# A's tile with its seven column groups side by side, late chunks' copies on ScalarE, and another written order, in a chunked RWKV-7 kernel with a SwiGLU feed-forward

## The chip, the core and the metric

The kernel runs on one core of one Trainium2 chip. The metric is the device time of one execution in microseconds, taken as the median of several runs. The core has five engines that run side by side, each through its own instruction list in order: TensorE (PE in the profile; its weight loads are PEld), VectorE (DVE), ScalarE (ACT), GpSimd (POOL) and SyncE (SP), of which SP only issues transfers. Transfers are also issued from POOL's queue.

## The reference

```python
# r, k, v, w, a, b: (B, H, S, D) = (4, 8, 768, 40), one state (D, D) per batch and head
for t in range(S):
    y[:, :, t] = einsum('bhd,bhde->bhe', r_t, state)
    Sa = einsum('bhde,bhe->bhd', state, a_t)
    state = state * w_t[:, :, None, :] - einsum('bhd,bhe->bhde', Sa, b_t) \
            + einsum('bhd,bhe->bhde', v_t, k_t)
x = y as (B*S, H*D) = (3072, 320)
xn = x / sqrt(mean(x*x) + 1e-6) * rms_g
out = (silu(xn @ w_gate) * (xn @ w_val)) @ w_out      # d_ff = 1536
```

All arithmetic is in 32-bit floats. The three weight matrices come in as 64-bit floats.

## The kernel before

The 768 steps are cut into 24 chunks of 32. The 32 pairs of batch and head lie side by side: `N = 8` slots times two halves, `NI = 16` on the free axis, the rest on the partitions.

`narrow` turns a weight slice's 64-bit words into 32-bit floats (three ACT passes and three DVE operations each for 24 half slices) and writes them to `sW` in memory, from which the feed-forward loads its tiles `wf`.

`front(c)` prepares chunk `c`: it loads and turns w, a, k and b. From them it builds products of decays `T`, the scaled keys `K` and the scaled `a` columns, and the matrix `LT` of what each step of the chunk does to later ones. `LT` is filled by distance. Columns up to three steps apart, within groups of four, come from one matmul group ("gramk") of `K` with the tile `A`; the levels 4, 8 and 16 come from three more with the tile `Ab`. For each of the 8 groups of four columns `A` has seven: the three a columns 1 to 3, two of them times a decay, and one of those times two; so its shape is [128, 16, 8, 7], the seven of a group next to each other. Line 742 (ACT) fills the first three, lines 751 and 752 (DVE) the others. Three masked copies (`where`, lines 757 to 760) take the product's columns for distance 1, 2 and 3 into `LT`, three, two and one column of each group. Line 770 (DVE) makes part of `Ab` from `A`.

`inverse(c)` inverts the chunk's triangular matrix: 31 steps of two small DVE operations each (`tmp`, `Yi`), with transfers before and after it. Chunks below `EARLY` use another form.

`main(c)` runs the chunk: "state" and "lower" matmuls, `Xs` (ACT), "lower" again into U, four copies of U into `VU` by half and slot group, "update" of the state, the turning of `VU`, "score", the masked scores `As` (one operation per level), "level" matmuls, sums into `y`, then the normalisation and the turn into `xg`. Some of these operations go to another engine from chunk `LATE` on.

`feed(g)` is the feed-forward for two chunks: six rounds of "h64", "h" (gate and value), Silu on ACT, a product on DVE (`hT`) and "out", summed in the PSUM tile `po`.

What comes when is written out by hand in ORDER. Every operation is a piece, numbered as the code makes it; a word of ORDER is a piece's number counted from the first piece not yet issued, so the words give each engine's order. A "-" issues a warm-up matmul (line 1079) on the identity into spare columns of `po`. PAIRS says for each PSUM room which of the three PSUM pairs it takes. Pieces wait for the pieces whose data they use, wherever these stand.

Of the kernel before, what the change touches and what calls it, by code (L numbers as in the profile page):

```python
# [17 lines left out]
P = 128  # L18
# [4 lines left out]
EARLY, LATE = 4, 6  # L23
# [10 lines left out]
4 5 6 7 8 9 10 11 - - 46 - - - - 43 53 18 - 316 323 58 - - 61 47 60 525 27 44 - - - - 12 13 14 15 16 17 19 317  # L34
- - 313 315 324 314 333 327 328 - 318 325 - 326 - - 73 339 - 74 85 93 84 - 94 82 83 334 337 - 336 335 338 -
340 349 20 21 22 350 355 23 342 343 24 25 26 - 367 - 354 348 - 352 - 344 345 363 346 365 347 - - 351 75 76 362
353 360 628 397 29 - 443 455 - 452 442 36 32 56 - 48 38 59 54 31 441 35 456 - 636 - 451 444 - 62 453 446 33 -
454 - 37 70 45 - 626 445 - 41 638 356 125 122 - 1 332 331 321 103 322 113 114 329 - 95 86 98 379 359 78 79 364
87 361 374 366 - 376 - 378 - - - - 373 77 357 368 371 377 375 387 372 89 88 358 - 461 - 386 369 383 90 80 -
380 381 465 370 466 384 - - 99 463 464 462 470 341 - 91 471 - - 478 - - 481 482 - 385 467 395 468 477 - - 476  # L40
- 483 493 480 - 389 391 390 - - 104 392 81 394 393 105 123 102 472 490 479 627 633 64 42 50 398 448 34 - 623 -
57 67 624 55 - 459 49 634 460 449 52 65 457 51 635 637 - - 473 - 474 491 - 475 450 - - 625 96 492 - 97 396 494
- - 489 - 504 382 100 487 488 - 484 506 - - 399 400 495 401 - 402 403 503 404 - - - 485 496 405 406 407 500
408 409 - 410 505 - 411 - 412 413 414 415 416 507 417 418 497 419 516 420 421 643 422 423 424 - 499 425 426
427 428 - 106 644 - - 502 501 498 107 108 429 124 320 0 317 90 576 - 132 577 - 328 99 643 645 511 510 - 484 -
113 646 644 509 107 - - - - 506 - 507 - 512 658 - 386 650 651 - 663 467 675 - - - 108 116 - 109 662 428 647
516 517 518 515 131 - 521 114 648 124 522 - 657 508 - - - 652 429 578 567 524 - - 61 870 456 861 860 - 640 66
445 430 69 - 598 871 26 - 28 64 639 630 67 629 110 519 520 434 656 - 653 - 654 661 - 117 660 659 127 128 - 655
580 - 115 - - 674 - - 579 513 664 - - - 432 143 431 433 118 525 526 670 568 125 126 669 133 581 666 134 135
435 436 437 438 569 141 142 140 119 687 129 - 668 673 667 161 152 151 163 - 665 144 527 528 529 136 137 138  # L50
679 530 531 532 533 671 534 535 536 537 147 676 160 130 573 571 572 570 672 682 145 146 684 148 538 680 539
540 541 542 543 544 545 546 547 548 149 549 550 685 551 552 553 - 554 582 583 686 - 574 153 555 575 681 156
677 162 139 801 164 678 586 688 167 157 689 - 589 595 590 - 604 693 154 165 155 690 587 588 596 1 0 962 135
145 144 113 146 134 663 519 661 662 560 136 137 143 612 121 122 660 556 557 555 646 554 712 520 664 665 562
129 138 655 147 148 149 563 131 564 568 565 132 569 - 713 566 832 668 33 - 827 841 826 825 - - 837 521 - 835
669 842 828 836 838 0 830 524 522 523 165 521 164 714 656 658 569 138 653 713 669 670 671 - 672 570 673 149
674 571 - 572 675 676 677 678 525 842 526 847 846 843 845 844 - 848 527 153 154 132 162 665 528 715 163 962
139 679 680 150 140 174 141 681 151 682 859 683 684 685 851 849 858 666 852 863 686 687 688 853 717 719 716
718 155 166 156 857 861 689 854 864 690 855 158 691 860 159 856 169 876 157 - 160 850 862 - 692 - 869 722 720
723 - - 546 764 182 - 152 183 185 173 167 547 726 573 168 875 574 - 721 - 575 729 731 865 1009 1008 - 600 -  # L60
1019 599 1018 1016 576 866 693 888 730 735 867 738 737 694 734 732 193 161 184 577 657 175 727 578 728 736 874
695 696 697 868 698 699 871 - 870 739 186 963 733 170 171 - 966 964 - 176 965 177 - 187 873 188 746 745 178
179 740 952 741 742 743 744 - 877 883 879 882 700 194 - - 579 881 880 747 180 872 887 886 172 195 885 580 748
582 - 878 889 891 581 884 749 750 751 752 753 829 590 589 1010 1020 896 754 892 - 890 1026 1013 1027 205 701
202 203 1021 1012 - 1022 - 1023 702 828 1028 705 703 950 951 755 - - 1011 894 893 838 756 1017 0 725 726 576
15 851 850 577 848 772 16 852 849 855 864 17 714 8 - 9 10 18 856 857 578 580 867 - 869 581 525 1093 579 19 23
33 719 720 32 853 723 854 868 862 863 877 866 879 523 717 0 573 515 575 516 713 869 517 847 707 710 711 574 42
0 509 5 839 840 845 841 707 861 567 753 850 14 754 855 856 755 893 568 708 709 569 570 757 853 710 - 711 8 17
851 712 713 714 715 716 717 718 854 719 871 523 21 23 22 867 852 858 756 - 872 - 766 868 524 - 866 869 873 720
# [4 lines left out]
776 876 877 878 18 879 880 881 882 883 884 885 748 - - 871 749 872 - - 1073 944 945 1078 1077 1075 1076 1074  # L74
23 560 719 561 1079 720 562 563 5 6 7 1082 1083 8 - 1090 886 887 1095 1093 1106 1080 947 564 0 12 715 24 - 712
556 13 16 1080 714 23 713 0 878 879 880 0 0 1072 875 1068 709 550 1069 1075 1070 876 1078 1087 877 710 10 1085
11 18 0 1073 1081 1080 9 875 1068 548 549 - - 708 - 1077 709 - 1085 1083 1079 - 929 758 759 876 1086 0 926
1077 17 1087 549 550 22 992 0 15 14 1193 12 542 543 544 765 1239 764 1250 1033 775 1043 867 868 869 1052 750
870 1090 871 872 1082 751 1240 920 1085 752 923 1089 1099 873 1083 874 875 876 1088 9 877 878 879 922 1084 921
545 1079 926 546 880 881 882 0 1085 1079 15 5 18 926 882 0 15 16 5 1079 545 546 1089 928 - 547 - - 548 - - -  # L80
939 1090 882 883 884 8 885 886 887 888 889 890 930 1093 1085 751 1091 929 1094 941 549 551 550 552 937 935 936
18 931 1092 19 891 932 553 938 940 892 893 894 895 896 897 933 898 899 900 942 554 555 1099 1098 1100 9 1101
972 - 0 1170 1083 1084 1085 0 196 546 - 0 0 385 343 344 551 - 386 - 345 552 376 346 - - 387 349 347 415 348
350 354 353 352 351 364 365 390 - 196 195 548 388 549 197 389 553 - 537 554 555 556 557 558 559 560 561 562
563 391 392 393 394 395 - 564 565 566 567 568 569 570 571 572 573 574 575 576 577 396 273 634 637 636 635 0 0
0 0 - 617 393 394 - 0 0 0 615 691 676 463 675 686 680 690 674 687 682 685 684 677 474 571 572 573 574 575 392
576 577 578 579 580 581 582 583 584 585 586 587 588 589 590 591 592 593 464 393 394 395 617 361 362 692 698
396 695 694 - 696 697 693 - - - 398 397 399 758 701 702 712 - 618 400 401 402 616 709 714 594 595 596 597 699
# [339 lines left out]
def kernel(  # L428
# [78 lines left out]
    def tt(o, a, b, op):  # L507
        dve("tt", nc.vector.tensor_tensor, o, a, b, op)
# [603 lines left out]
```

## Time and profile before

| | |
|---|---|
| runs, median of 3 | 1048.17 us (1045.47 to 1050.28) |
| profiled execution, span from first to last instruction | 1035.9 us |
| median of the runs less the span | 12.3 us |
| mean granted TensorE clock | 0.972 |
| instructions | 56007 |
| PE busy, matmuls | 989.6 us, 96% |
| DVE busy | 832.1 us, 80% |
| ACT busy | 450.8 us, 44% |
| POOL busy | 309.1 us, 30% |
| transfers from memory and back | 93.39 MB and 15.99 MB |
| copy of the first and the last group's `po` | at 232.3 and 1030.8 us |

The profiled execution's time is known only as its span; the 12.3 us are what lies around the span by the runs. Rows of instruction groups read: line, engine, operation, out<-in, shapes, count | busy us, mean ns of one | idle us just before them and what ended it. Rows of windows read: from:to, length, busy us of the engines (with counts), granted clock, share of the transfer engines, GB/s. Rows of the chain and of the timeline begin with the start and the length in us. All operations of one helper have its line: 505 is any DVE operation, 528 an ACT copy, 531 an ACT scaling, 547 a matmul, 550 a turn.

### The profile page before, as it was taken

Reading aid. Unit: us, or ns where it says so; the run is one execution under the profiler, and the core shown is the slowest. Engines: PE = TensorE matmul, PEld = TensorE weight load, DVE = VectorE, ACT = ScalarE, POOL = GpSimd, SP = SyncE. Lnnn points to the kernel's source line nnn. Section 1 sums busy time; section 2 is a strip of 40 time slices with the busy share of each in tenths; the row PEclk is TensorE's granted clock in tenths of the full one; section 3 lists DMA queues with packets and bytes.
Section 4 is the critical chain, followed back from the end, with each engine's and each line's share of the span. In section 5 each row is a group of like instructions: output and inputs, shape, how many; then the busy total and the mean of one; then the engine's idle time right before and its main releaser. Section 6 shows DMA issues by size and latency. Waiting matters only on the chain.

```text
span 1035.9 us, 56007 instructions
## 1 busy us (share of the span) xinstructions
PE 989.6 (96%) x24842; PEld 807.6 (78%) x24842; DVE 832.1 (80%) x2789; ACT 450.8 (44%) x1019; POOL 309.1 (30%) x554
## 2 busy tenths in 40 slices
PE   7987999999999999999999999999999999999998
PEld 7976877788887787787877787887787877778876
DVE  8987688686869899899989888888799898788410
ACT  5784775543553443443443433452434444341210
POOL 9633413041442233232244232333232432210000
PEclk9976699999999999999999999998999999999999
DMA  8877356755442634434443535334633624422222
GB/s 161 158 194 171 97 158 165 202 131 127 105 87 64 145 79 103 120 65 106 101 98 83 143 75 125 87 68 99 133 62 68 162 65 107 114 51 54 89 77 65
DMA packets 163538, 113.03 MB, mean 109 GB/s; under 512 B 124512, under 2 KB 142880, under 8 KB 163296
## 3 DMA queue, kind: packets, MB, share of 16 engines
q1 hardware_dynamic: 144928, 86.48, 33.8%
q0 software_dynamic: 16192, 22.64, 11.3%
q8 instruction: 195, 3.19, 1.3%
q10 hardware_dynamic: 2176, 0.33, 0.3%
q14 instruction: 47, 0.39, 0.1%
HBM read 93.39 MB, written 15.99 MB: 106 GB/s over the span
## 4 chain that ended last, share of the span: by engine, by line
PE 54%; DVE 30%; issue 5%; DMA 5%; ACT 3%; SPq 2%; POOL 1%; DVEq 0%; ACTq 0%; POOLq 0%
PE ps L547 36%; PE po L547 10%; DVE tmp L505 5%; DVE Yi L505 5%; PE ps L550 5%; DVE LT L505 4%; PE po L1079 3%; DVE K L505 3%; DVE As L505 2%; SPq L544 2%; DVE Ab L505 1%; DVE hT L505 1%; DMA wf<-sW 1%; DVE y L505 1%; DVE T L505 1%
## 5 line engine op out<-in xcount | busy, mean ns | idle before, releaser
L547 PE MATMUL ps<-xg,wf 128*128 128x256 f32 (+1 forms) x1728 | 353.8, 391 | 1.1 <-DMA wf<-sW 0.7
L547 PEld LDWEIGHTS ps<-xg,wf 128*128 128x128 f32 (+1 forms) x1728 | 263.1, 190 | 50.6 <-issue 15.2
L547 PE MATMUL po<-wf,hT 128*128 128x320 f32 x576 | 177.0, 445 | 0.1
L505 DVE TENSOR_TENSOR tmp<-Yi,M 128x60 f32<-128x60 f32 (+24 forms) x620 | 130.3, 210 | 19.8 <-DMA M<-sB 5.4
L505 DVE TENSOR_TENSOR Yi<-Yi,tmp 128x60 f32<-128x60 f32 (+24 forms) x620 | 129.8, 209 | 14.6
L525 ACT ACTIVATE sg<-ps 128x512 f32<-128x512 f32 x72 | 43.0, 597 | 216.5 <-PE ps L547 216.3
L547 PEld LDWEIGHTS po<-wf,hT 128*128 128x128 f32 x576 | 104.6, 191 | 37.0 <-issue 2.1
L544 POOL DMA_DIRECT2D kbn<-in_b_dram x92 | 53.8, 587 | 191.7 <-PE ps L547 169.9
L528 ACT COPY KN<-ps 128x640 f32<-128x640 f32 x96 | 66.3, 692 | 88.0 <-DVE LT L505 50.5
L505 DVE TENSOR_TENSOR K<-K,T 128x512 f32<-128x512 f32 (+1 forms) x192 | 94.0, 496 | 3.4 <-ACT K L528 2.7
L1079 PE MATMUL po<-ident 128*128 128x128 f32 x522 | 92.5, 313 | 3.3 <-DVE po L579 3.3
L505 DVE TENSOR_TENSOR hT<-ps,sg 128x512 f32<-128x512 f32 x72 | 49.6, 689 | 51.6 <-ACT sg L525 51.0
L528 ACT COPY K<-K 128x256 f32<-128x256 f32 (+1 forms) x168 | 72.6, 444 | 35.2 <-DVE K L505 25.0
L547 PEld LDWEIGHTS ps<-Ab,K 40*60 40x60 f32 (+2 forms) x4608 | 68.7, 129 | 19.7 <-issue 6.5
L505 DVE TENSOR_TENSOR As<-ps,msi 128x256 f32<-128x256 f32 (+1 forms) x186 | 82.9, 478 | 1.1 <-PE ps L547 0.6
L547 PE MATMUL ps<-Ab,K 40*60 40x56 f32 (+2 forms) x4608 | 78.2, 217 | 5.2 <-DVE K L505 2.5
L1079 PEld LDWEIGHTS po<-ident 128*128 128x128 f32 x522 | 73.9, 208 | 11.5 <-POOL wan L540 3.3
L544 POOL DMA_DIRECT2D VU<-in_v_dram x92 | 53.8, 586 | 93.5 <-PE ps L550 55.9
L547 PEld LDWEIGHTS ps<-As,KN 128*40 128x40 f32 x3072 | 68.1, 128 | 13.9 <-issue 8.4
L544 POOL DMA_DIRECT2D wn<-in_w_dram x92 | 51.9, 566 | 90.0 <-DVE KN L505 56.4
L547 PE MATMUL ps<-As,KN 128*40 128x32 f32 x3072 | 74.0, 208 | 3.7 <-issue 1.5
L544 POOL DMA_DIRECT2D kbn<-in_k_dram x92 | 53.4, 583 | 76.7 <-PE ps L547 73.3
(137 smaller groups left out, 1470.3 us busy)
## 6 DMA issues: line engine op xcount, KB each, us to landing
wf<-sW SPq DMA_DIRECT2D x82, 480.0 KB, 4.4
M<-sB SPq DMA_DIRECT2D x80, 128.0 KB, 3.6
rn<-in_r_dram SPq DMA_DIRECT2D x24, 160.0 KB, 5.0
out_dram<-o SPq DMA_DIRECT2D x48, 80.0 KB, 3.2
kbn<-in_b_dram POOLq DMA_DIRECT2D x92, 40.0 KB, 3.1
kbn<-in_k_dram POOLq DMA_DIRECT2D x92, 40.0 KB, 3.2
wan<-in_a_dram POOLq DMA_DIRECT2D x46, 80.0 KB, 3.7
wan<-in_w_dram POOLq DMA_DIRECT2D x46, 80.0 KB, 4.3
```

Source lines behind the costliest of these rows:

```text
L505: plan.add("DVE", kind, lambda at: fn(at(o), *m(at)), [o], aps(*args))
L525: plan.add("ACT", "act", lambda at: nc.scalar.activation(at(o), at(a), f, **kw), [o] + aps(acc), [a])
L528: plan.add("ACT", "copy", lambda at: nc.scalar.copy(at(o), at(a)), [o], [a])
L544: plan.add(by, "dma", lambda at: queue.dma_start(out=o, in_=i), [o], [i])
L547: return o, lhsT, rhs, lambda at: nc.tensor.matmul(at(o), lhsT, rhs, start=start, stop=stop, skip_group_check=True)
L550: return o, i, ident, lambda at: nc.tensor.transpose(at(o), i, ident)
L1079: plan.warm = lambda: nc.tensor.matmul(po_[:, 0, DM:DM + P], ident, ident, start=False, stop=False, skip_group_check=True)
```

## The change

There are three edits.

1. `A` becomes [128, 16, 7, 8]: all eight groups of one of the seven columns lie next to each other. The views of the copies, products and masked copies that write or read it are turned accordingly, and so is the order of the matmul's columns. The number of operations is the same.
2. `LATE` becomes 24, which no chunk reaches; the one use that scales `xg` gets a 6 in its place. So from chunk 6 on the two U copies that were on DVE, the copy of swapped r halves (each second chunk) and the level-16 mask (two scalings instead of one product) are on ACT.
3. ORDER and PAIRS are written anew. ORDER has 26 "-" instead of 261.

```diff
-EARLY, LATE = 4, 6
+EARLY, LATE = 4, 24
...
 ORDER = """
...
 PAIRS = """
...
-    A_ = Turns(1, [P, NI, 8, 7], "A", whole)
+    A_ = Turns(1, [P, NI, 7, 8], "A", whole)
...
-            copy(A[:, i::2, :, 0:3], a4.rearrange("p n (g j) -> p n g j", j=4)[:, :, :, 1:4])
+            copy(A[:, i::2, 0:3], a4.rearrange("p n (g j) -> p n j g", j=4)[:, :, 1:4])
...
-        w4 = Tl[1].rearrange("p n (g j) -> p n g j", j=4)
-        tt(A[:, :, :, 3:5], A[:, :, :, 1:3], w4[:, :, :, 1:3], MUL)
-        tt(A[:, :, :, 6], A[:, :, :, 4], w4[:, :, :, 1], MUL)
+        w4 = Tl[1].rearrange("p n (g j) -> p n j g", j=4)
+        tt(A[:, :, 3:5], A[:, :, 1:3], w4[:, :, 1:3], MUL)
+        tt(A[:, :, 6], A[:, :, 4], w4[:, :, 1], MUL)
...
-                        A[part(o), 2 * n + i].rearrange("p g j -> p (g j)")) for n, i, o in each])
-        g4 = gr.rearrange("p o n t -> p (o n) t")[:, :, 0:56].rearrange("p n (g j) -> p n g j", j=7)
+                        A[part(o), 2 * n + i].rearrange("p j g -> p (j g)")) for n, i, o in each])
+        g4 = gr.rearrange("p o n t -> p (o n) t")[:, :, 0:56].rearrange("p n (j g) -> p n j g", j=7)
         for dist, at in ((1, 0), (2, 3), (3, 6)):
             m = 4 - dist
-            where(LT.rearrange("p n (g j) -> p n g j", j=4)[:, :, :, dist:], near[:, dist - 1:dist].rearrange(
-                "p u (g j) -> p u g j", j=4)[:, :, :, dist:].bitcast(U32).to_broadcast((P, NI, 8, m)), g4[:, :, :, at:at + m])
+            where(LT.rearrange("p n (g j) -> p n j g", j=4)[:, :, dist:], near[:, dist - 1:dist].rearrange(
+                "p u (g j) -> p u j g", j=4)[:, :, dist:].bitcast(U32).to_broadcast((P, NI, m, 8)), g4[:, :, at:at + m])
...
-            tt(Ab[:, :, 16 * x:16 * x + 16].rearrange("p n (h j) -> p n h j", j=4)[:, :, :, 1:4], A[:, :, x::2, 0::3],
-               w4[:, :, x::2, 0:1].to_broadcast((P, NI, 4, 3)), MUL)
+            tt(Ab[:, :, 16 * x:16 * x + 16].rearrange("p n (h j) -> p n j h", j=4)[:, :, 1:4], A[:, :, 0::3, x::2],
+               w4[:, :, 0:1, x::2].to_broadcast((P, NI, 3, 4)), MUL)
...
-        if c < LATE:
+        if c < 6:
             for kt in range(KT):
                 scale(xt[:, :, kt], ps[:, :, kt], gcol[:, kt:kt + 1])
```

The other three uses of `LATE` stand unchanged in the code: line 893 (U), line 913 (r) and line 929 (the mask).

More of the change, by code (lines that the diff above doesn't have):

```diff
@@ new lines @@
+600 138 139 485 162 164 137 140 - 496 512 511 498 497 508 510 525 513 431 509 643 873 644 648 647 517 645 649 523
[5 rows of a table added]
+183 685 627 693 553 554 - 176 588 555 182 595 678 878 556 174 677 688 689 604 - - 590 699 175 177 698 869 592 697
[3 rows of a table added]
+21 516 - 517 14 17 685 518 519 0 403 844 4 31 509 7 356 374 21 510 5 846 404 405 543 511 484 375 493 836 687 545
[4 rows of a table added]
+541 542 543 544 545 812 657 802 494 24 0 0 799 626 491 809 - 660 811 544 739 654 545 546 14 741 665 0 542 670 663 1
[3 rows of a table added]
+683 684 828 803 722 723 685 686 687 688 689 492 493 - 541 664 807 808 426 724 725 726 9 809 690 691 810 1052 1001
[5 rows of a table added]
@@ new lines @@
+839 772 1044 537 538 539 843 1046 844 15 845 1043 1048 840 1047 913 1049 914 972 - 916 841 917 846 847 1237 848
[8 rows of a table added]
+552 345 346 553 554 621 635 622 194 349 347 537 388 555 556 557 558 559 624 392 195 560 348 197 561 393 350 394 -
[3 rows of a table added]
+- 621 622 732 620 401 737 734 402 733 580 0 580 729 716 402 730 715 403 726 727 738 728 581 582 739 408 749 583 584
[4 rows of a table added]
+778 937 956 963 828 779 780 829 974 938 781 610 2 947 609 945 - 413 744 782 831 414 632 973 420 783 421 611 936 958
[17 rows of a table added]
+559 539 409 535 321 358 359 543 546 545 360 361 362 363 415 556 - 0 0 550 357 358 359 533 0 359 408 533 360 542 545
[10 rows of a table added]
@@ new lines @@
+229 4 234 340 342 344 341 5 0 5 230 529 231 0 0 323 335 229 17 0 321 171 172 - 173 174 175 176 177 178 8 221 231 17
[17 rows of a table added]
+846 847 440 677 678 777 551 679 680 681 682 441 444 953 778 779 780 969 781 962 963 632 629 973 952 - 683 436 974
[3 rows of a table added]
+443 992 450 463 857 996 1003 999 1000 993 810 1013 706 811 812 1008 813 455 - 456 814 815 816 817 818 1007 1009 819
[9 rows of a table added]
+604 - 605 0 753 754 639 752 605 606 756 764 607 433 432 734 776 608 609 745 746 751 757 758 610 611 612 747 - 767
+769 766 768 429 636 - 759 434 387 651 1 773 435 613 614 615 616 617 618 643 388 706 666 652 655 657 772 761 668 -
@@ new lines @@
+619 763 969 644 660 968 430 436 437 707 663 669 - - 771 770 658 446 656 849 438 659 662 667 620 621 622 623 624 625
[16 rows of a table added]
+628 668 959 760 771 664 669 - 656 657 660 772 665 670 773 671 667 672 673 770 675 955 454 763 674 954 1 626 676 952
+627 448 777 963 778 779 780 781 443 444 677 782 629 783 784 785 450 678 679 786 787 753 680 681 451 - 788 633 953
[8 rows of a table added]
+715 720 - 557 559 721 710 547 717 558 728 733 718 562 726 699 494 425 637 551 553 563 722 727 729 737 561 730 738
[37 rows of a table added]
+616 617 654 665 655 768 959 618 619 668 - 620 621 667 767 438 439 436 765 656 766 771 696 769 958 440 772 762 658
[20 rows of a table added]
@@ L261 @@
+2120200012012022210012211010212002012121001122102202001011110020120212002120001212120012212210101211011112221002120
+2002022220011200020001201111022122220220102020200002202201012101111211221222022022010020022002021000121011122122221
+1022000012102012011121000100010110121021101210211211102110222020221010100212010012112101122112101120001020212021222
+201200222101001012120201110221222102121
 """
```

121 lines of the change are left out of this document (3 added, 118 removed), and 287 rows, old and new, of the table ORDER.

## The prediction

> **What bounds the kernel now.** I read the page first: its span, the engines' totals, the clock in 40 slices and the chain that ended last.
>
> ```profile
> span 1035.9 us, 56007 instructions
> PE 989.6 (96%) x24842; PEld 807.6 (78%) x24842; DVE 832.1 (80%) x2789; ACT 450.8 (44%) x1019; POOL 309.1 (30%) x554
> PEclk9976699999999999999999999998999999999999
> PE 54%; DVE 30%; issue 5%; DMA 5%; ACT 3%; SPq 2%; POOL 1%; DVEq 0%; ACTq 0%; POOLq 0%
> L547 PE MATMUL ps<-xg,wf 128*128 128x256 f32 (+1 forms) x1728 | 353.8, 391 | 1.1 <-DMA wf<-sW 0.7
> L547 PE MATMUL po<-wf,hT 128*128 128x320 f32 x576 | 177.0, 445 | 0.1
> L1079 PE MATMUL po<-ident 128*128 128x128 f32 x522 | 92.5, 313 | 3.3 <-DVE po L579 3.3
> ```
>
> PE looks full, but the group of line 1079 does nothing for the result: it is the warm-up matmul that each "-" of ORDER issues. The old ORDER has 261 such words (I counted them in the text), and 522 rows are two per word. So useful PE time is 989.6 - 92.5 = 897.1 us, and 1035.9 - 897.1 = 138.8 us are lost: 92.5 as warm-ups, 46.3 idle. The feed-forward alone is 353.8 + 177.0 = 530.8 us of PE that no edit here touches. The new ORDER has 26 "-".
>
> Next, the windows: all instructions in five stretches, then the warm-ups (line 1079) in the same stretches, PE first in each row, the granted clock behind the engines.
>
> ```profile
> 0.00:60.00 60.00, 52.47 (x1231) 48.77 (x1232) 54.91 (x157) 39.68 (x84) 45.94 (x100) 0.99 0.79 158
> 60.00:130.00 70.00, 59.03 (x1765) 52.62 (x1764) 50.41 (x154) 46.59 (x103) 24.08 (x47) 0.67 0.62 155
> 130.00:230.00 100.00, 93.62 (x2433) 76.14 (x2435) 81.38 (x276) 56.49 (x126) 26.31 (x46) 0.98 0.65 166
> 230.00:960.00 730.00, 712.97 (x18678) 575.47 (x18667) 629.01 (x2169) 295.90 (x685) 211.68 (x361) 1.00 0.43 97
> ```
> ```profile
> 0.00:60.00 60.00, 35.66 (x258) 32.26 (x258) 0.99 0.79 158
> 60.00:130.00 70.00, 18.96 (x76) 14.45 (x76) 0.67 0.62 155
> 130.00:230.00 100.00, 13.09 (x78) 10.40 (x77) 0.98 0.65 166
> 230.00:960.00 730.00, 24.81 (x112) 16.84 (x112) 1.00 0.43 97
> ```
>
> The head, up to 230 us, has 205.12 us of PE busy, of which 67.71 are warm-ups: 137.4 useful, 92.6 lost. But there DVE is as good as full at first (54.91 of 60), and weights are still being narrowed: PE is not what sets the head's pace, so its warm-ups mostly fill waits. In the steady stage, 230 to 960 us, PE is busy 712.97 of 730, of which 24.81 are warm-ups: 688.2 useful, 41.8 lost. DVE is at 629.0 of 730, 86%. How many chunks pass there, one row tells (the transposed U's copy, one per chunk):
>
> ```profile
> L528 ACT COPY vut<-ps x20: 1005/1012/1022, 236.9 to 967.1; 128x1024 f32<-128x1024 f32 x20
> ```
>
> Nineteen intervals in 730.2 us are 38.4 us per chunk, of which 688.2 / 19 = 36.2 are useful PE work and 33.1 DVE work. **PE is the floor of the steady stage**; 2.2 us per chunk stand above it. The part after 960 us is the last feed-forward groups; I leave it as it is.
>
> **The change, part by part. A's layout.** Lines 742, 751 to 760 and 770 keep their instruction counts; only the inner runs change, from 3, 2 or 1 elements to 8 (4 in line 770). PE reads the same 56 columns. Now the rows by form:
>
> ```profile
> L505 DVE COPY_PREDICATED LT<-near,ps 128x384 f32<-128x384 uint32 x24 | 17.5, 728 | 5.3 <-PE ps L547 5.0
> L505 DVE COPY_PREDICATED LT<-near,ps 128x128 f32<-128x128 uint32 x24 | 17.4, 726 | 0.2
> L505 DVE COPY_PREDICATED LT<-near,ps 128x256 f32<-128x256 uint32 x24 | 17.4, 725 | 0.3
> L505 DVE COPY_PREDICATED LT<-msk,ps 128x256 f32<-128x256 uint32 x72 | 30.9, 429 | 14.6 <-PE ps L547 7.0 <-ACT KN L528 6.9 <-issue 0.3
> L505 DVE TENSOR_TENSOR As<-ps,msi 128x256 f32<-128x256 f32 x144 | 57.0, 418 | 1.1 <-PE ps L547 0.6 <-ACT As L531 0.2 <-ACT KN L528 0.2
> L505 DVE TENSOR_TENSOR As<-ps,msi 128x512 f32<-128x512 f32 x42 | 28.5, 684 | 0.0
> L505 DVE TENSOR_TENSOR Ab<-A,T 128x192 f32<-128x192 f32 x48 | 21.1, 443 | 0.2
> L505 DVE TENSOR_TENSOR A<-A,T 128x128 f32<-128x128 f32 x24 | 9.6, 400 | 0.4
> L505 DVE TENSOR_TENSOR T<-T 128x128 f32<-128x128 f32 x24 | 6.9, 286 | 0.2
> ```
>
> The three near-diagonal copies cost the same 0.73 us whether 384, 256 or 128 elements are copied. What they share is 128 short runs (16 heads by 8 groups). The masked copy in runs of 4 and longer takes 429 ns for 256 elements, and 684 - 418 = 266 ns per 256 further elements is 1.04 ns each. With runs of 8 I therefore estimate 429 + 133 = 562, 429 and 429 - 133 = 296 ns, 1.29 us against 2.18: 0.89 us less per chunk. The other bound is no gain (the output and the mask now go in steps of 4, and no masked copy of the trace does that); I take the estimate, since the ns per run fit. Line 770 by the same slope is 418 - 67 = 351 ns instead of 443, twice, and the 128x128 product 286 instead of 400: 0.3 us more (between 0 and that). ACT's two copies of A stay. Sum: DVE 1.2 us per chunk less, 29 us in all.
>
> **LATE from 6 to 24.** Line 997 keeps its 6, but three lines change for the 18 chunks from 6 on: 893 (two U copies of the second half of heads), 929 (the level-16 mask: one DVE product becomes two ACT scalings) and 913 (the swapped r, each second chunk two). The new ORDER has 5,888 words beside the "-", 18 more than the old: that is line 929's extra piece.
>
> ```profile
> L505 DVE COPY VU<-ps 32x320 f32<-32x320 f32 x36 | 17.3, 480 | 6.9 <-ACT VU L528 6.2 <-PE ps L547 0.2
> L528 ACT COPY VU<-ps 32x320 f32<-32x320 f32 x60 | 25.0, 417 | 23.1 <-PE ps L547 11.7 <-DVE VU L505 10.4
> L505 DVE COPY r<-ps 64x512 f32<-64x512 f32 x18 | 12.4, 689 | 2.6 <-PE ps L550 1.5 <-ACT rE L528 0.7
> L528 ACT COPY r<-ps 64x512 f32<-64x512 f32 x6 | 3.5, 580 | 2.5 <-PE ps L550 2.4
> L531 ACT ACTIVATE As<-ps,msi 128x256 f32<-128x256 f32 x12 | 5.5, 471 | 7.2 <-DVE As L505 4.8 <-PE ps L547 2.4
> ```
>
> DVE loses 36 x 0.480 + 18 x 0.689 + 18 x 0.684 = 42.0 us; ACT gains 36 x 0.417 + 18 x 0.580 + 36 x 0.471 = 42.4. Per late chunk that is 2.3 us each way. DVE falls from 832 to about 761 us, ACT rises from 451 to 493: half idle still, so its throughput hides this. In the steady stage DVE goes from 33.1 to 29.6 us per chunk, 77% of 38.4. The moved work keeps its place in the chunk, but four U copies now stand in line on one engine: two more behind two, 0.83 us later in the worst case, before "update" and the turn of VU may begin. What covers it is the feed-forward matmuls that PE has between "lower" and "update" in its order; without cover it costs up to 0.8 us per chunk.
>
> A rule speaks against these moves. In the Trainium skill, "ScalarE: Activation LUTs", section "Rules for kernel authors", multiplications are to go to VectorE and not to ScalarE, which is put at up to about three times slower for bf16. Here the rows settle it: from PSUM and in f32, the copies are faster on ACT (417 against 480 ns, 580 against 689); only the mask agrees with the rule (2 x 471 against 684). At the rule's factor of three a U copy would take ACT 3 x 480 = 1440 ns, an estimate from that page, the two more in line 2.9 us per chunk, and the 17 chunks of the second rival below would cost about 50 us instead of 19; the rows say no such thing, and the sum goes by them.
>
> **The order, and 235 fewer warm-ups.** At 92.5 / 261 = 0.354 us each, 83.3 us leave PE. In the first tenth of the words the old order has 133 "-", the new has 5. That bounds the effect: if every removed warm-up had filled a wait, nothing is gained (0); if each had delayed something, 83. For the head I take nothing. The chain holds a few, but others stand at waits that stay, and without them the clock falls, which is priced below. Two early rows of the chain of waits show the size:
>
> ```profile
> 20.26 1.98 PE po L1079 x16
> 24.23 0.64 PE po L1079 x4
> ```
>
> So the head gets only A's layout: six fronts x 1.2 us, half of it on a DVE that is 81% busy there (186.7 of 230), -4 us; and +2 for PE's useful work in the first 60 us at a lower clock (16.8 us of it, most behind DVE). In the steady stage 41.8 us are lost. These are waits for other engines that the warm-ups cover up, and DVE, whose share of the chain is 30%, gives back 3.5 of 33.1 us per chunk. I take one third of the loss, 14 us: the DVE idle time of a chunk goes from 5.3 to 8.8 us, so queueing behind it should shrink by about a third. Sum: 1035.9 - 4 + 2 - 14 = 1020 us of span. The runs' median, 1048.17, lies 12.3 us above the profile's span, and that difference stays: **1032 us**, 1.5% faster.
>
> **Rivals.** First, slower: the clock. It is PE's clock in the head. Two windows of ten microseconds, and from the timeline of PE the same matmul group at two clocks and the first matmuls of the feed-forward:
>
> ```profile
> 50.00:60.00 10.00, 7.78 (x293) 7.09 (x290) 9.17 (x25) 8.37 (x17) 5.57 (x11) 0.95 0.60 150
> 110.00:120.00 10.00, 9.87 (x216) 8.70 (x209) 9.23 (x27) 7.91 (x17) 0.90 (x3) 0.50 0.40 104
> 13.17 1.15 PE L547 MATMUL ps<-A,K 40*64 40x56 f32 x64
> 95.20 1.97 PE L547 MATMUL ps<-A,K 40*64 40x56 f32 x64
> 132.19 1.11 PE L547 MATMUL ps<-xg,wf 64*128 64x256 f32 x8
> ```
>
> Up to 60 us the dense warm-ups hold it at 0.99; then it falls to 0.67 though PE stays 84% busy, and small groups take 1.97 instead of 1.15 us. If the new order's PE is too sparse until 230 us, the stretch 130:230, with 80.5 us of useful PE at 0.98, runs at the 0.67 of the stretch before: 80.5 x 0.98 / 0.67 = 118 us, 18 over its 100. It decides from a mean clock of about 0.8 there, where 80.5 us becomes the whole 100. With the steady stage no better, since cold spells there eat the gain: 1048 + 18 = 1066. For it: nearly all warm-ups of the head go. Against it: at 110:120 the clock was 0.50 with PE 9.87 busy, so warm-ups did not hold it; and the feed-forward, which begins at 132 us, brings it to 1.00 by itself. The Trainium skill, "TensorE: Matmul & The Clock Gate", Part 1, says the same: the gate gives half rate by default, full rate after about 3.4 us of sustained activity, half again after an idle window of that length. By that rule a sparse head is cold throughout and the feed-forward is not.
>
> Second, slower: the chunk's serial path. U's four copies on ACT (+0.83) and the mask as two scalings (2 x 0.471 - 0.684 = +0.26) lengthen the way from "lower" to "level" by 1.1 us; if it ends last in PE's fixed order, 17 late chunks cost +19 and DVE's relief is worth nothing: 1048 + 19 = 1067. The point is where no ready feed-forward matmuls stand between. Against it: of the steady stage's 17 us of idle PE, hardly any row names ACT.
>
> ```profile
> PE ps L547 <- issue: 8.8, 10, 2.4
> PE ps L547 <- DVE As L505: 1.0, 3, 0.5
> PE ps L547 <- ACT VU L528: 0.2, 1, 0.2
> ```
>
> Third, nothing: PE is at its floor, the waits behind the warm-ups come from DMA round trips and code ("issue"), and removed warm-ups turn into idle: 1048, less the head's 2, plus some of the first two: 1046. Fourth, more gain: two thirds of the steady loss and a few of the head's warm-ups go: 1032 - 14 - 8 = 1010. That the relayout doesn't do what it says (0.73 us stays) is part of the third: DVE then keeps 22 of the 71 us.
>
> **How the numbers follow.** Forecast 0.42, fourth case 0.12, third 0.13, clock 0.19, serial path 0.14. A measurement can tell about 0.5%, 5.2 us, from no change; the first two cases are faster than that, the third lies within, the others beyond: 0.54, 0.13, 0.33. The range reaches from 1007 (the fourth case; 1048 less the whole steady loss is 1006) to 1068 (both slower cases); the faster cases alone would hold 1007 to 1042.
>
> **What would show it.** Near-diagonal copies falling with their size (about 0.56, 0.43, 0.30 us); DVE near 761 and ACT near 493 us; about 52 rows of line 1079; useful PE time still near 897 us, or more if the clock fell; vut copies 37.7 us apart. I am wrong on the order if the interval is 38.4 or more, on the head if the first o copy comes later than now by over 5 us, and on the clock if the stretch 130:230 is granted less than 0.8.

## The result, and the profile after

The changed kernel is slower: 1094.53 us (median of 4 runs, 1093.32 to 1096.64) against 1049.22 us of the kernel before beside it (4 runs, 1045.47 to 1052.47). The ratio is 1.0447, 95% interval 1.0417 to 1.0477. The forecast was 1032, its range 1007 to 1068. Medians and ranges here and below are of all runs; a ratio leaves out runs more than 1.5% above the fastest of their kernel.

The page of the changed kernel, its span, the engines, the clock and the chain that ended last:

```profile
span 1094.9 us, 55087 instructions
PE 966.3 (88%) x24372; PEld 785.0 (72%) x24372; DVE 850.0 (78%) x2717; ACT 490.8 (45%) x1109; POOL 309.4 (28%) x554
PEclk9998679798989999999999988999999999999999
PE 61%; DVE 22%; issue 7%; ACT 4%; DMA 4%; POOL 1%; SPq 0%; DVEq 0%; ACTq 0%; POOLq 0%
```

ACT went from 450.8 to 490.8 us, as forecast (493). DVE should have fallen to 761 and rose from 832.1 to 850.0. The rows by form of the changed kernel tell why (line 489 is now any DVE operation, 512 an ACT copy, 515 an ACT scaling, 531 a matmul):

```profile
L489 DVE COPY_PREDICATED LT<-near,ps 128x384 f32<-128x384 uint32 x24 | 44.8, 1868 | 3.9 <-PE ps L531 3.8
L489 DVE COPY_PREDICATED LT<-near,ps 128x256 f32<-128x256 uint32 x24 | 31.0, 1293 | 0.4
L489 DVE COPY_PREDICATED LT<-near,ps 128x128 f32<-128x128 uint32 x24 | 17.3, 722 | 0.3
L489 DVE TENSOR_TENSOR Ab<-A,T 128x192 f32<-128x192 f32 x48 | 25.0, 530 | 0.3
L489 DVE TENSOR_TENSOR A<-A,T 128x256 f32<-128x256 f32 x24 | 14.9, 622 | 0.3 <-ACT A L512 0.2
L512 ACT COPY VU<-ps 32x320 f32<-32x320 f32 x96 | 40.0, 417 | 25.3 <-PE ps L531 23.8
```

The near-diagonal copies do cost by their size now, but upwards: 1868, 1293 and 722 ns, where 562, 429 and 296 were forecast and 728, 725 and 726 stood before. They alone add 93.1 - 52.3 = 40.8 us.

Where the time went, by two events: the first copy of `po`, which ends the head, and the last one.

```profile
L512 ACT COPY o<-po x12: 682/690/697, 266.8 to 1089.5; 128x640 f32<-128x640 f32 x12
L512 ACT COPY vut<-ps x24: 1006/1012/1030, 81.4 to 1026.9; 128x1024 f32<-128x1024 f32 x24
```

Before, the `po` copies went from 232.3 to 1030.8 us. So of the span's 59.0 us more, 34.5 are in the head and 24.2 between the two copies. (The medians differ by 45.3 us only: before's profiled execution was one of its faster ones.)

PE's account shows the same 59.0 us in another way. The 26 "-" left 52 rows of warm-ups, as forecast:

```profile
L1063 PE MATMUL po<-ident 128*128 128x128 f32 x52 | 14.1, 373 | 0.0
```

So 78.4 us of warm-ups are gone. But PE's idle time rose by 82.3 us, from 46.3 to 128.6, and the same 24320 useful matmuls held PE for 966.3 - 14.1 = 952.2 us instead of 897.1, 55.1 more (49 if each group's own time is added up, since neighbours overlap a little). The prediction had named this sign of a fallen clock.

The windows of the changed kernel and its waits of PE (total, times, longest, in us), with the row of `LT` in the kernel before as the last:

```profile
0.00:60.00 60.00, 24.18 (x676) 21.50 (x676) 47.19 (x127) 32.75 (x68) 39.57 (x88) 1.00 0.86 178
60.00:130.00 70.00, 50.29 (x1664) 45.39 (x1659) 59.59 (x172) 47.28 (x104) 26.42 (x51) 0.80 0.64 152
130.00:230.00 100.00, 81.31 (x2297) 65.87 (x2290) 69.32 (x193) 52.20 (x116) 26.71 (x48) 0.85 0.52 128
230.00:960.00 730.00, 681.47 (x17466) 550.70 (x17465) 611.96 (x2044) 322.97 (x750) 212.12 (x361) 0.96 0.42 96
```
```profile
PE ps L531 <- issue: 30.3, 26, 4.6
PE ps L531 <- DVE LT L489: 13.5, 8, 2.5
PE ps L531 <- DVE K L489: 12.8, 5, 6.6
PE ps L547 <- DVE LT L505: 0.6, 3, 0.2
```

PE now waits for `LT`, the very tile that the dear copies fill, and its granted clock in the steady stage is 0.96 instead of 1.00. The `vut` copies of that stage, 19 intervals from 271.1 to 1026.9 us, are 39.8 us apart instead of 38.4: over the bound at which the prediction meant to be wrong on the order. (The clock of the first two rows is not to be believed, see the last section.)

### The profile page after: what moved, and what is told of

It reads as the page before. It is cut to its first block, busy times and chain, and to the rows that moved or that the text cites. A ratio compares the mean times of both kernels' runs of the same rounds, so it can differ in the third digit from the quotient of the medians.

```text
span 1094.9 us, 55087 instructions
## 1 busy us (share of the span) xinstructions
PE 966.3 (88%) x24372; PEld 785.0 (72%) x24372; DVE 850.0 (78%) x2717; ACT 490.8 (45%) x1109; POOL 309.4 (28%) x554
## 4 chain that ended last, share of the span: by engine, by line
PE 61%; DVE 22%; issue 7%; ACT 4%; DMA 4%; POOL 1%; SPq 0%; DVEq 0%; ACTq 0%; POOLq 0%
PE ps L531 43%; PE po L531 12%; DVE LT L489 7%; PE ps L534 5%; DVE K L489 3%; DVE tmp L489 2%; DVE Yi L489 2%; DVE Ab L489 1%; ACT K L512 1%; DVE y L489 1%; DMA wf<-in_moe_w_out_dram 1%; DVE hT L489 1%; POOL kbn L528 1%; DVE As L489 1%; DMA kbn<-in_k_dram 1%
## 5 line engine op out<-in xcount | busy, mean ns | idle before, releaser
L531 PE MATMUL ps<-xg,wf 128*128 128x256 f32 (+1 forms) x1728 | 374.8, 408 | 9.4 <-issue 5.1
L531 PEld LDWEIGHTS ps<-xg,wf 128*128 128x128 f32 (+1 forms) x1728 | 277.1, 199 | 61.3 <-issue 16.2
L531 PE MATMUL po<-wf,hT 128*128 128x320 f32 x576 | 182.7, 454 | 6.0 <-issue 3.4
L531 PE MATMUL ps<-Ab,K 40*60 40x56 f32 (+2 forms) x4608 | 85.2, 229 | 33.4 <-DVE K L489 12.8
L531 PEld LDWEIGHTS ps<-Ab,K 40*60 40x60 f32 (+2 forms) x4608 | 75.6, 140 | 49.6 <-issue 21.8
L489 DVE COPY_PREDICATED LT<-near,ps 128x384 f32<-128x384 uint32 (+2 forms) x72 | 93.2, 1294 | 4.6 <-PE ps L531 3.8
L489 DVE TENSOR_TENSOR As<-ps,msi 128x256 f32<-128x256 f32 (+1 forms) x168 | 70.0, 458 | 21.7 <-ACT As L515 16.4
L489 DVE TENSOR_TENSOR y<-y,ps 128x256 f32<-128x256 f32 x119 | 50.0, 420 | 24.9 <-PE ps L531 21.3
```

Of the source, the lines that this page charges most:

```text
L489: plan.add("DVE", kind, lambda at: fn(at(o), *m(at)), [o], aps(*args))
L531: return o, lhsT, rhs, lambda at: nc.tensor.matmul(at(o), lhsT, rhs, start=start, stop=stop, skip_group_check=True)
```

## The experiments

Each is given as median, with the range, and its ratio to the kernel before on the same chip, with the 95% interval. **Parts of the change alone.** The first keeps before's order and LATE and takes only the new layout of `A`.

```diff
-    A_ = Turns(1, [P, NI, 8, 7], "A", whole)
+    A_ = Turns(1, [P, NI, 7, 8], "A", whole)
     (and the views of lines 742 to 770, as in the change)
```

> The order, PAIRS and LATE of before; only A's layout is new. Theory 1 (the layout is the loss): the three near-diagonal copies take 1.87, 1.29 and 0.72 us as in the changed kernel, and A's and Ab's products 0.62 and 0.53; that is 2.0 us more DVE per chunk, 48 us in all (832 to about 880), and since DVE was at 86% in the steady stage and nearly full in the first 60 us, the time rises by 20 to 45 us, 1069 to 1094. Theory 2 (the order is the loss): the copies get longer as well, but PE has other work, and the time stays within 10 us of 1049.

Measured: 1093.36 us (1091.38 to 1097.92), 1.0435 [1.0366, 1.0505]. The layout alone costs as much as the whole change.

The second takes only LATE 24, in before's order, with the 18 added scalings right behind their twins.

```diff
-EARLY, LATE = 4, 6
+EARLY, LATE = 4, 24
```

> The order of before, with the 18 extra scalings put right behind their twins, the layout of before; only LATE is 24. DVE 832 to 790 us, ACT 451 to 493. Theories 1 and 2 both put no loss here: 1039 to 1052. Theory 3 (the longer serial path on ACT): 1060 to 1068.

Measured: 1061.72 us (1058.90 to 1068.71), 1.0137 [1.0063, 1.0212]. The groups that moved took 41.8 us off DVE, as the prediction's rows said (42.0; DVE's total fell by 36.5), and the kernel became slower. In its profile PE waits 20.6 us for ACT in all, instead of 4.7. Some of it is for the U copies, which had 0.4 us before, and more for the copies `KN`, which were on ACT already and had 0.5 (544 is a matmul here, 547 a turn):

```profile
PE ps L544 <- ACT KN L525: 7.9, 7, 4.0
PE ps L544 <- ACT VU L525: 2.4, 2, 1.4
PE ps L547 <- ACT VU L525: 2.1, 5, 1.0
```

The third takes only the new ORDER and PAIRS, less the 18 added words.

```diff
 ORDER = """
-(the old words)
+(the new words, 18 fewer)
```

> The order and PAIRS of the changed kernel without the 18 extra scalings, the layout and LATE of before. Theory 2: the time is 1075 to 1095, the first chunk's keys arrive late (turned at about 20 us instead of 11), and the clock drops every few tens of us in the steady stage. Theory 1: 1040 to 1060.

Measured: 1107.53 us (1092.09 to 1109.59), 1.0483 [1.0356, 1.0610]. The new order without the moves is about as bad as the layout.

The fourth is the change without the layout.

```diff
-    A_ = Turns(1, [P, NI, 7, 8], "A", whole)
+    A_ = Turns(1, [P, NI, 8, 7], "A", whole)
     (and the views, as before; ORDER, PAIRS and LATE as changed)
```

> The changed kernel with A's old layout: near-diagonal copies at 0.73 us each, DVE 850 to about 803. Theory 1: 1050 to 1065, most of the 45 us come back. Theory 2: 1080 to 1094, DVE had room.

Measured: 1047.80 us (10 runs, 1037.55 to 1055.22), 0.9970 [0.9926, 1.0013]. Order and LATE, harmful one by one, together make no difference; the 47 us that are left are the layout's. Against the third experiment, from which this kernel differs by LATE and its 18 words, the moves take 39.9 us off DVE (841.1 to 801.2) and are worth some 50 us; in the old order they cost 12. Its page, its windows from 130 us on, its wait for `LT` and its `po` copies:

```profile
span 1047.1 us, 55087 instructions
PE 947.1 (90%) x24372; PEld 772.6 (74%) x24372; DVE 801.2 (77%) x2717; ACT 491.5 (47%) x1109; POOL 309.6 (30%) x554
130.00:230.00 100.00, 84.04 (x2236) 67.39 (x2230) 66.56 (x203) 52.21 (x114) 27.02 (x47) 0.87 0.55 137
230.00:960.00 730.00, 701.49 (x18463) 570.29 (x18462) 607.94 (x2157) 338.69 (x784) 210.17 (x359) 0.99 0.43 97
PE ps L531 <- DVE LT L489: 1.8, 3, 0.7
L512 ACT COPY o<-po x12: 684/690/697, 253.0 to 1041.7; 128x640 f32<-128x640 f32 x12
```

Between this span and the changed kernel's lie 47.8 us, and PE accounts for both halves: the same 24372 matmuls took 966.3 - 947.1 = 19.2 us longer, at a lower clock (0.96 against 0.99 in the steady stage), and PE stood idle for 128.6 instead of 100.0 us, 28.6 more. By the `po` copies the layout adds 13.8 us in the head and 34.0 behind it. Against before's profile, the order with LATE costs 20.7 us in the head and wins 9.8 behind it; but that profile is of an execution some 10 us faster than before's median, and a fairer pair follows under "The head".

**Why the layout is dear.** A kernel of its own times masked copies by their pattern, eight of each: the old and the new ones, and 384 elements with a step or in runs on one side alone.

```diff
+copies(step(target("outstep4", 96), 4), bc(m1[:, :, 0:24], (P, 16, 24)), flat(g))
+copies(flat(target("maskstep4", 24)), bc(step(m1, 4), (P, 16, 24)), flat(g))
+copies(flat(target("instep2", 24)), bc(m1[:, :, 0:24], (P, 16, 24)), step(g, 2))
 ...
```

> A kernel that computes none of the reference: 8 masked copies in a row of each pattern, tile by tile (old3 to old1: the old patterns, new3 to new1: the new ones, and one step at a time; 384 elements where no number says otherwise). If a step in the written tile is what costs, outstep4 and outstep2 take about 1.87 us and maskstep4 and instep2 about 0.56; if it is the mask's step, maskstep4 takes 1.87 and outstep4 0.56; if each run of contiguous elements costs about 4.5 ns whatever its length up to 4, run2of, run4of and run8of take about 1.0, 0.58 and 0.55 us. The product with a step of 4 in its output stays at the dense one's time, as the K products of the kernel did.

Measured, by form (behind the bar: busy us, mean ns of one; "run2of" writes runs of two in every four, "run8of" runs of eight in every sixteen):

```profile
L39 DVE COPY_PREDICATED new<-mask,gr 128x384 f32<-128x384 uint32 x8 | 14.7, 1843 | 0.0
L39 DVE COPY_PREDICATED new<-mask,gr 128x256 f32<-128x256 uint32 x8 | 10.4, 1304 | 0.0
L39 DVE COPY_PREDICATED old<-mask,gr 128x384 f32<-128x384 uint32 x8 | 5.7, 719 | 0.2
L39 DVE COPY_PREDICATED old<-mask,gr 128x128 f32<-128x128 uint32 x8 | 6.1, 757 | 0.1
L39 DVE COPY_PREDICATED run2of<-mask,gr 128x384 f32<-128x384 uint32 x8 | 8.0, 1004 | 0.2
L39 DVE COPY_PREDICATED run8of<-mask,gr 128x384 f32<-128x384 uint32 x8 | 4.5, 558 | 0.2
L39 DVE COPY_PREDICATED dense<-mask,gr 128x384 f32<-128x384 uint32 x8 | 4.9, 609 | 0.2
L39 DVE COPY_PREDICATED maskstep<-mask,gr 128x384 f32<-128x384 uint32 x8 | 6.6, 828 | 0.2
L39 DVE COPY_PREDICATED instep<-mask,gr 128x384 f32<-128x384 uint32 x8 | 4.6, 580 | 0.2
```

The view of one tile, here the copies that write in steps of four and of two, has the least, the median and the most ns of one; the most is step four, the least step two:

```profile
L39 DVE COPY_PREDICATED outstep<-mask,gr x16: 1005/1532/1855, 64.6 to 86.7; 128x384 f32<-128x384 uint32 x16
```

What counts is how many groups of four neighbouring floats (16 bytes) the copy comes to while it writes. In the changed kernel's order of elements it comes to a new one with every element: 384, 256 and 128 of them for 1868, 1293 and 722 ns, that is 4.5 ns per group and some 150 ns besides. By that, the old copies visit 128 groups each, whether they write three, two or one of the four: 150 + 128 x 4.5 = 726 ns, all three. Runs of two in every four, or a step of two, visit 192: 1014 (measured 1004 and 1005). Dense, or in runs of eight, there are 96: 582 (609 and 558). Counting stretches of neighbouring elements instead does not fit: a step of two makes 384 of them, one element each, and takes no longer than 192 runs of two. A step of four in the mask costs 0.2 us, a step of two on the read side nothing.

Two more kernels test this in place. One is the kernel with the old layout and the new order, with only the loops of the three masked copies turned: the same elements to the same places, eight groups of a column at a time.

```diff
-            where(LT.rearrange("p n (g j) -> p n g j", j=4)[:, :, :, dist:], ... g4[:, :, :, at:at + m])
+            where(LT.rearrange("p n (g j) -> p n j g", j=4)[:, :, dist:], ... g4[:, :, at:at + m])
```

> The changed order and LATE with A's old layout (1048 us), and only the three masked copies walk as in the changed kernel: eight groups innermost, written in steps of 4, read from the old columns of the product in steps of 7. If the step of the written side is the whole cause, the copies take 1.87, 1.29 and 0.72 us and the time is 1085 to 1095, all of the loss without the new tile; if the products on A and Ab or the matmul carry a share, 1060 to 1080.

Measured: 1090.89 us (1082.97 to 1097.95), 1.0436 [1.0371, 1.0502].

```profile
PE 966.0 (88%) x24372; PEld 783.4 (71%) x24372; DVE 842.5 (77%) x2717; ACT 490.9 (45%) x1109; POOL 308.9 (28%) x554
L489 DVE COPY_PREDICATED LT<-near,ps 128x384 f32<-128x384 uint32 x24 | 44.9, 1871 | 6.5 <-PE ps L531 6.3
```

That is 43 us over the same kernel without the turn, for 41.3 us more of DVE, and by the ratios (1.0436 and 1.0447) the whole loss of the changed kernel within the noise. So the turned loops of these copies are the loss; that it is their written side, and not the mask or the source, rests on the probe.

The other is the changed kernel with `A` side by side, from which the matmul reads the columns in the old sequence, so that the old masked copies fit.

```diff
-                        A[part(o), 2 * n + i].rearrange("p j g -> p (j g)")) for n, i, o in each])
+                        A[part(o), 2 * n + i].rearrange("p j g -> p g j")) for n, i, o in each])
     (and the masked copies as before)
```

> The changed kernel with A's new layout, but the matmul reads A's columns so that the product comes out in the old sequence, and the three masked copies are the old ones (0.73 us each). If the masked copies are the cause, 1045 to 1062, with about 8 us more DVE time than with the old layout; if the tile's layout costs by itself, 1075 to 1095.

Measured: 1059.77 us (1054.22 to 1063.41), 1.0152 [1.0106, 1.0199].

```profile
L489 DVE COPY_PREDICATED LT<-near,ps 128x384 f32<-128x384 uint32 x24 | 17.5, 728 | 9.1 <-PE ps L531 8.9
L531 PE MATMUL ps<-A,K 40*64 40x56 f32 x1536 | 45.3, 283 | 1.6 <-issue 1.1 <-ACT K L512 0.3
```

The copies are at 728 ns again, and by the medians 35 of the 47 us are back (by the ratios to before, each on its own chip, 31 of 50). The 12 to 19 left have two candidates, not told apart: the matmuls that now read `A` in steps (45.3 us, against 31.5 in the changed kernel), and the products into `A` and `Ab`, some 8 us dearer.

**How the time answers to DVE.** 41 us more on an engine that is 77% busy cost 43. To see whether that is special to the near copies, the kernel of the new order and old layout gets each of them twice, which changes nothing in `LT`,

```diff
-            where(LT..., near..., g4...)
+            where2(LT..., near..., g4...)     # the same copy issued twice
```

> The changed order and LATE with A's old layout (1047.8 us before), each near-diagonal copy issued twice in its place: 2.18 us more DVE per chunk, 52 in all, nearly what the new layout added. Theory A (what counts is the place: these copies stand on DVE ahead of products that the next matmul group of the front waits for): 1085 to 1100. Theory B (DVE load as such): also 1080 to 1100. Theory C (the new layout costs through something else than its DVE time): 1047 to 1060.

or, elsewhere in the chunk, the product that decays the state four times over.

```diff
-            tt(Sdec, ST..., z["T"][32]..., MUL)
+            (the same product issued four times)
```

> The same base, with the product Sdec issued four times instead of once: 2.45 us more DVE per chunk, 56 in all, at a place that only the state's update waits for. Theory A: 1047 to 1065. Theory B: 1080 to 1100, as with the doubled copies.

Measured: 1112.67 us (1102.34 to 1115.80), 1.0624 [1.0534, 1.0714], and 1100.61 us (1093.35 to 1105.71), 1.0513 [1.0411, 1.0615].

```profile
PE 978.4 (88%) x24372; PEld 793.3 (71%) x24372; DVE 854.2 (77%) x2789; ACT 491.6 (44%) x1109; POOL 309.3 (28%) x554
```
```profile
PE 966.3 (88%) x24372; PEld 783.1 (71%) x24372; DVE 857.6 (78%) x2786; ACT 491.6 (45%) x1109; POOL 309.3 (28%) x554
```

53.0 us more of DVE cost 65 us, 56.4 us cost 53. DVE work that is added in either place is paid about one for one; so the price isn't special to the place of `LT`. In both, PE's waits for DVE rise, from 14 to 54 and 59 us, and its matmuls take 31 and 19 us longer.

**The head.** The changed order loads the first keys late: five of ACT's eight transfers of `kbn` stand behind its first copies, which wait for the turned `wan`, and PE waits 12.3 us for one. The next kernel (new order, old layout) has all eight first.

```diff
 ORDER = """
-(ACT's eight kbn loads spread over the first words)
+(the eight first, the rest in the same sequence)
```

> The same base, with ACT's eight loads of the first chunk's keys issued ahead of its first copies, as in the order of before; nothing else moves. The keys should be turned at about 11 us instead of 20; if the head's loss of 21 us is that wait, the time falls by 8 to 12 us, to 1036 to 1040; if the weight slices' transfers or the clock set the head, by less than 3.

Measured: 1049.59 us (10 runs, 1038.25 to 1055.58), 0.9998 [0.9945, 1.0051]. The late keys don't set the head. Its profiled execution is as long as before's, 1036.4 against 1035.9 us, and so the fairer pair:

```profile
L518 ACT COPY o<-po x12: 684/692/698, 250.2 to 1031.1; 128x640 f32<-128x640 f32 x12
```

The first `po` copy comes 17.9 us later than before, and the stretch from there to the last is 17.6 us shorter. What the new order with LATE wins in the steady stage, it loses in the head.

Then the kernel before without its 261 warm-ups,

```diff
 ORDER = """
-(old words with 261 "-")
+(old words without a "-")
```

> The kernel before without any of its 261 warm-ups, all else the same. If they only fill waits (the prediction's reading), the time stays within 10 us of 1048 and 92 us of PE busy vanish; if they hold the clock that the head needs, the head (to the first copy of o, at 232 us) is 10 to 20 us longer and the clock is 0.5 in most of the first 130 us: 1058 to 1070; if they stood in the way, 1000 to 1035.

and the new order (old layout) with 214 of the old head's warm-ups put back.

```diff
 ORDER = """
+(214 "-" more in the head)
```

> The changed order and LATE with A's old layout (1048 us), with the old order's 214 warm-ups of the head put ahead of the same matmul groups, up to the end of the first feed-forward group. If the clock makes the new head 21 us longer (253 to the first copy of o instead of 232), 1028 to 1038; if it is the order of the other engines' work, 1043 to 1053.

Measured: 1082.84 us (1082.76 to 1087.46), 1.0341 [1.0294, 1.0389], and 1108.15 us (1103.60 to 1108.91), 1.0563 [1.0515, 1.0612]. The windows of the first, from 130 us on:

```profile
130.00:230.00 100.00, 83.95 (x2121) 65.71 (x2122) 69.30 (x229) 49.28 (x107) 17.59 (x31) 0.85 0.59 150
230.00:960.00 730.00, 686.04 (x17700) 546.51 (x17696) 606.14 (x2094) 292.05 (x680) 215.72 (x368) 0.97 0.43 94
```

So the warm-ups were worth some 36 us in the order that held them. The clock falls from 0.98 to 0.85 at 130 to 230 us and from 1.00 to 0.97 in the steady stage, and the same 24320 useful matmuls hold PE for 963.6 us instead of 897.1. The `po` copies go from 245.3 to 1076.0 us, so most of the loss lies behind the head. But they are no cure elsewhere: in the new order the clock of that stretch stays at 0.86, and each warm-up stands ahead of work:

```profile
130.00:230.00 100.00, 87.76 (x2312) 71.70 (x2306) 63.17 (x188) 51.44 (x112) 25.97 (x46) 0.86 0.51 124
230.00:960.00 730.00, 680.07 (x17388) 552.25 (x17382) 575.36 (x2025) 319.62 (x741) 212.58 (x364) 0.97 0.43 95
```

The same with warm-ups later: the changed kernel with 72 more, one ahead of each of the four product groups of every `front` from chunk 6 on.

```diff
 ORDER = """
+(72 "-", ahead of the "gramk" groups from chunk 6 on)
```

> The changed kernel, with one warm-up ahead of each of the four product groups of every front from chunk 6 on, 72 in all (25 us of PE), where PE now waits for DVE. If the lost 45 us are partly the clock (56 us at half speed behind 230 us, against 19 with the old layout), that time falls below 30 us and the run to 1075 to 1088; if the waits for DVE alone carry it, 1090 to 1100; if the warm-ups delay the groups, above 1100.

Measured: 1130.33 us (1128.49 to 1147.44), 1.0810 [1.0763, 1.0857].

Last, two attempts to take the good of each: the old order to the end of the first feed-forward and the new one from there, with the old layout and LATE 24,

```diff
 ORDER = """
-(new words to the end of feed 0)
+(old words to the end of feed 0)
```

> A's old layout and LATE 24, the words of the old order up to the end of its first feed-forward group and then what is left in the new order's sequence. If head and steady stage add up, the first copy of o comes at 232 us and the other eleven follow within 790: 1022 to 1035. If the steady stage's gain hung on what the new head had prepared, 1045 to 1060.

and the same with the scalings of `xg` on ACT as well, for all chunks.

```diff
-        if c < 6:
+        if c < NCH:
             for kt in range(KT):
                 scale(xt[:, :, kt], ps[:, :, kt], gcol[:, kt:kt + 1])
```

> The kernel of e11_old_head, with the scaling of xg by gcol on ACT for all chunks (three ACT scalings of 0.39 us instead of one DVE product of 0.56 us in 18 chunks): DVE 10 us less. By the runs before, in which 50 us more on DVE cost 50 to 65 us, it should be 8 to 12 us below e11_old_head; if DVE's relief gives nothing any more, equal or up to 10 us slower.

Measured: 1048.66 us (1039.33 to 1054.16), 0.9995 [0.9930, 1.0061], and 1067.39 us (1061.53 to 1072.32), 1.0181 [1.0125, 1.0237]. The first gives the head back (first `po` copy at 238.1 instead of 253.0 us) and loses as much behind it (808.8 us to the last one, against 788.7). The second takes 6.5 us more off DVE and costs 19. No kernel that was run beats the kernel before by what can be measured.

## Why the prediction was wrong, step by step

**A's layout, the term that failed.** The step is the estimate of 1.29 us per chunk for the near copies, and its bound: "The other bound is no gain". It measured 1868 + 1293 + 722 = 3.88 us. The three equal rows of 0.73 us were read as 128 short runs, which longer runs would cure. But the view turns the loops, and `LT` stays as it was: the eight elements of a "run" lie four floats apart, so what became long is the loop and not the stretch that is written. The prediction saw that step of 4, had no row of it, and let it cost nothing, where nothing excluded a loss. Two of its rows would have given the size: the copy in runs of four and longer comes to 64 groups of four floats in 429 ns, the near copies come to 128 in 726, and the line through both gives, as an estimate, 1.9 us at the 384 groups that came after. The Trainium skill, "SBUF — State Buffer", "Specifications (TRN2)", has the rule that was missed: memory lines are of 16 bytes, and full bandwidth needs at least two accesses on each. The runs agree for one access per line (1855 ns in steps of four, against 609 dense). For two they do not, and the measurement decides: 1005 ns is still far from 609. On DVE the term was worth +40.8 us instead of -21.

**The products into A and Ab** were to gain 0.3 us per chunk. They lost 0.34: 622 instead of 450 ns, and twice 530 instead of 443, less 10 ns of the third. The first now reads the decays in steps of four floats, and the twins write `Ab` in such steps, a new group with each element; no run takes these patterns apart.

**LATE.** The durations were right (417, 581 and 474 ns, ACT +40.0 us). The worth was not: in the old order the moves cost 12.3 us, and PE's waits for ACT rose by 15.9. That is near the second rival, which had 19 us, but only 4.5 us of the waits name U's copies, as it had it, and 7.9 the `KN` copies that share ACT with them. With the new order PE's waits for ACT are 11.4 us, none of them for U, and the moves pay. The rule against ScalarE in the Trainium skill, "ScalarE: Activation LUTs", "Rules for kernel authors", was rightly set aside for the copies: 417 ns for a U copy, in 96 rows of it.

**"PE is the floor of the steady stage", DVE has slack.** Adding DVE work, at either place tried, costs about its own length. Taking it away gives nothing in the old order (the second experiment) and nothing in the last one, where ACT took over; in the new order the same moves are worth some 50 us (the third against the fourth). So the price of DVE time hangs on the order it stands in. With the order of each engine fixed in writing, a longer operation pushes what PE does behind it, at that place, whatever the engine's share over the span; DVE's 30% of the chain was the hint. The step by which DVE gives back 3.5 us per chunk and queueing "should shrink by about a third" took the average for the place. And a gap in PE seems to cost twice: the 28.6 us of idle PE came with 19.2 us of slower matmuls. The Trainium skill, "TensorE: Matmul & The Clock Gate", Part 1, puts the gate at half rate after an idle window; the clock of 0.96 instead of 0.99 in the steady windows is in keeping with it.

**The head, "I take nothing" for the warm-ups.** Off by 18 to 21 us by the order with LATE alone. In the old order the warm-ups do hold the clock (0.98 with them, 0.85 without, from 130 to 230 us), as the first rival had it, against the argument that the feed-forward restores the clock by itself. In the changed kernel that stretch stands at 0.85 too, so by the prediction's bound of 0.8 this rival would not count. The bound was too low: without warm-ups the old order's head was some 13 us longer at that same 0.85. How much of the new head's 18 to 21 us is clock and how much is the written order stays open: putting warm-ups back makes the new order slower by 60 us.

**The steady stage's -14.** The order and LATE gave -9.8 us between the first and the last `po` copy in one execution and -17.6 in the one that is as long as before's, near the forecast; but a third of the relief behind that forecast, 1.2 of 3.5 us of DVE per chunk, was to come from the layout and did not, so the agreement is partly luck. The layout took the gain and more. By the medians: order and LATE together make no difference, the layout costs 47 us.

**The 12.3 us between span and median** are no overhead. The changed kernel's profiled execution took 1096.64 us at a span of 1094.9, 1.7 more; the profile of before was merely one of that kernel's faster executions, which in thirteen runs beside the probe took 1038.9 to 1056.4. The sum should have said that it starts 10 us low; adding the 12.3 at the end made this good by luck.

The fourth rival, more gain, found no support in any run. The third, nothing, is what order and LATE gave together (0.9970), and its removed warm-ups that turn into idle time are what PE's account shows (78.4 us gone, 82.3 us more idle), though it allowed for a relayout that does nothing and not for one that harms.

## What to carry to other kernels

Turning the loops of a masked copy on VectorE doesn't make its runs longer unless the memory that is written is turned too; count the 16-byte groups that it comes to in order, and price those. Where the trace has no row for a new pattern, the bound has to reach to the loss. In a kernel whose engines each follow a written order, an engine's share of busy time says little of what one more microsecond on it costs: double one operation and measure.

## What the runs showed of the hardware

- A masked copy (VectorE, 32-bit) takes about 150 ns and 4.5 ns for each 16-byte group that it visits while writing, full or not: 722 ns at 128, 1004 at 192, 1293 at 256, 1868 at 384. A plain product in the probe suffers less: 960 ns with the written side in steps of four floats, 713 dense. Both alternated with copies, and their length changed with the copy (the dense one took 0.59 to 0.76 us), so this is rough.
- A matmul whose moving operand is read eight floats apart is slower: the same 1536 matmuls had PE busy for 45.3 instead of 31.5 us.
- The clock in the records can't be trusted ahead of its first entry, which in the changed kernel comes at 98.4 us. The first row of its windows says 1.00 up to 60 us, but a matmul group inside it has the length that it had at half clock in the prediction's rows:

```profile
22.98 1.97 PE L531 MATMUL ps<-A,K 40*64 40x56 f32 x64 [1.15 <-issue]
```
